# A Fourier mixing and feed-forward kernel: the head's loads, its d=128 transform and its weight products in another order

## The chip, the cores and the metric

One Trainium2 chip (trn2), one of its cores. The metric is the device time of one execution in microseconds, as the median of several runs. A profiled execution gives the spans, the rows and the waits that this text reads.

## What is computed

```python
def _attn_ref(x):                       # x: (8, 3008, 256) float32
    X = np.fft.fft(x, axis=1)
    X = np.fft.fft(X, axis=2)
    return X.real.astype(np.float32)

def _moe_ref(x, w_in, w_out):           # x: (24064, 256), w_in: (256, 2048), w_out: (2048, 256)
    h = x @ w_in
    g = np.maximum(0.01 * h, h)
    return (g @ w_out).astype(np.float32)
```

The real part of a two-dimensional Fourier transform of each batch goes, as 24064 rows of 256, through a layer of 2048 hidden units with a leaky ReLU and back to 256. `w_in` and `w_out` come as 64-bit floats, and the kernel makes 32-bit floats of them itself.

## The kernel before

**The mathematics.** The transform over the 256 features is never carried out on the data. It is multiplied into the first weights: `fold_w_in` makes `wf`, the product of a cosine and sine table (`feat_sb`) with `w_in`, in two halves, `wf[:, 0]` for the cosines and `wf[:, 1]` for the sines. Row 0 of the sine half holds the weights of feature 128, the nyquist feature of the feature axis (the "d=128" column); `spread_wn` sends these by small DMAs to `wn`, one column for each 128 hidden units. The transform over the 3008 sequence positions uses all its symmetries: the input is laid out with mirrored rows, `add_mirrors`, `fold_columns` and `fold_halves` add and subtract them on VectorE, and for even frequencies `fold_quarters` folds once more. What is left is a short product with a table (`sequence`: four matmuls of even rows into `pe`, three of odd rows into `po`), and `butterfly` puts the two sums together on ScalarE and VectorE as a tile `mix`.

**The units.** A unit is a batch and a parity of the frequency (odd first). Each has two mixes, block 0 for the cosines and block 1 for the sines; `dft` makes one. The d=128 column of all eight batches has a transform of its own (`nyquist`), with 8 rows instead of 128; its result is kept in DRAM and spread to all partitions by `spread`, or for the first unit by two matmuls with a row of ones (`spread_first`).

**The steps.** A unit's columns come in three blocks `j` of 251 or 250. `up(j, f)` multiplies two blocks of 128 hidden units (four matmuls into `cos_ps` and `sin_ps`), adds the d=128 column (L543), forms both signs (L547, L548) and applies the leaky ReLU (L549). `down` multiplies by `w_out`, with seven products instead of eight by a Strassen-Winograd scheme (L601), or plainly in the first two blocks (`down_plain`, L581). Here `f` runs over 8 pairs of hidden blocks. In the first two blocks the pair is `(2f, 2f+1)`, so that the steps need `wf` in rising order of columns.

**The head.** The first 16 steps are written out by hand, since they run while the weights still arrive. `load_w_in` and `load_w_out` issue loads on SP; `Weights.begin`, `mantissa` and `end` turn 64-bit words into 32-bit floats on VectorE (L343, L344, L351, L361, L362) with two steps on ScalarE (L345, L346); `convert_on(old, new)` runs the end of one conversion with the beginning of the next. `fold_w_in` is called five times: columns 0 to 255, 256 to 511, then three times 512 columns (`WN`). Each call makes the sine half's product first (L393), copies it on ScalarE (L394), issues the rows of `wn` (L401), then the cosine half's. `keep_warm(n)` issues `n` matmuls on a tile of zeros.

**What sets the order.** Inside the `with` block the order on VectorE, TensorE and SP is the one written, and in the inner block that of POOL too; ScalarE's is chosen by a scheduler when the program is built. After the block the scheduler orders all engines, by the order written and by what its own model takes to be ready, and it may put such later instructions between those of the block: the small quarter folds of the d=128 column (L274 to L280 on `nyx`), which are written after the block, stand on VectorE near 15 us. Loads share one queue on SP. Eight semaphores count their landings in turn, so a load also waits for the landing of the eighth before it. The PSUM tag `up` has four banks, used in turn by up steps, transforms and weight products; the tag `sum` has four for the down steps and the warming matmuls.

The lines that the prediction follows: L393 and L394 (weight products and copies), L401 (rows of `wn`), L431 and L441 (even and odd rows of a transform), L482 to L484 (the d=128 fold on POOL), L538 (up), L581 (plain down).

Of the kernel before, what the change touches and what calls it, by code (L numbers as in the profile page):

```python
# [48 lines left out]
F32 = mybir.dt.float32  # L49
# [6 lines left out]
P = 128  # L56
# [3 lines left out]
NT = 7  # L60
# [144 lines left out]
def tile_fnet_leaky_relu(  # L205
# [98 lines left out]

    def load_tab(q, n, c):
        t = const.tile([P, TW[c][n % 2]], F32, name=f"tab_{n}_{c}")
        q.dma_start(t, seq_tab[n, c, :, 0 : TW[c][n % 2]])
        tabs[n, c] = t
# [78 lines left out]

    def fold_w_in(f0, n, made):

        for w in (1, 0):  # L390
            pt = up_ps()[:, 0:n]
            for a in range(2):
                nc.tensor.matmul(pt, lhsT=feat_sb[:, a, w * P : (w + 1) * P], rhs=made[a].dst, start=(a == 0), stop=(a == 1))  # L393
            nc.scalar.copy(wf[:, w, f0 : f0 + n], pt)  # L394
            if w == 1:
                spread_wn(f0, n)
# [18 lines left out]

    def sequence(rows, m, part, c):

        pe, po = dft_ps(), dft_ps()  # L420
        kf, kw = KF[c], KW[c]
        tab, n = tabs[2 * part, c], NI[0]
        for i in range(n):
            if c == 1:
                still, to = rows[0:PE_ROWS, i], pe[0:m, i % 2 * kf : (i % 2 + 1) * kf]
            else:
                q, p = divmod(i, 2)
                still, to = rows[0][(p + part) % 2][0:PE_ROWS, q], pe[0:m, q * kf + p : (q + 1) * kf : 2]
            at = i * TW[c][0] // n

            nc.tensor.matmul(to, lhsT=still, rhs=tab[0:PE_ROWS, at : at + to.shape[1]],  # L431
                             start=(i == 0), stop=(i == n - 1), skip_group_check=True)
        tab, n, at = tabs[2 * part + 1, c], NI[1], 0
        for i in range(n):
# [8 lines left out]
            at += to.shape[1]  # L443
        return pe, po

# [12 lines left out]

    def dft(u, blk):


        b, c = u
        if u in folded:
            rows = folded[u][blk]
        elif c == 1:
            rows = zs[b][:, 1 - blk, 0, :, blk * P : (blk + 1) * P]
        else:
            rows = quarters.pop((b, blk))
        sums = sequence(rows, P, blk, c)

        def rest():
            t = work.tile([P, UW[0]], F32, tag=f"mix{blk}", bufs=2, name=f"mix{blk}")
            butterfly(t, sums, P, blk, c)
            mixed.setdefault(u, {})[blk] = t
        return rest

# [8 lines left out]

    def nyquist(c):
        if c == 1:
            rows = nya[:, 1]
        else:
            halves = [nyb[:, 0], nyb[:, 1]]  # L490
            fold_quarters(nya[:, 0], halves, halves[0][:, 5], [h[:, 6] for h in halves])
            rows = halves, halves[0][:, 5]
        sums = sequence(rows, B, 0, c)

        def rest():
            t = work.tile([P, UW[0]], F32, tag="mix0", bufs=2, name="nyq")
            butterfly(t, sums, B, 0, c)
            nc.sync.dma_start(nyq_dram[:, c, 0 : UW[c]], t[0:B, 0 : UW[c]])
            return t
        return rest  # L500

# [115 lines left out]
    def step(at):  # L617
        if at < len(steps):
# [6 lines left out]
            if n == 0 and f in (2, 5):  # L625
                dft(units[1], f // 5)()
            if 0 < n < len(units) - 1 and f == 4:
                if part == 0:
                    spread(units[n + 1])
                    if n % 2 == 1:  # L630
                        fold_x(b + 1)
                else:
                    dft(units[n + 1], part - 1)()
            if n % 2 == 0 and part == 2 and f == 6 and b + 1 < B:
# [5 lines left out]
    xs = {}  # L640

    def convert_w_in(f0, n, made):
        convert(made)
        fold_w_in(f0, n, made)

# [6 lines left out]
    with tc.manual_schedule(engines={mybir.EngineType.DVE, mybir.EngineType.PE, mybir.EngineType.SP}):  # L652
        with tc.manual_schedule(engines={mybir.EngineType.Pool}):
# [56 lines left out]
        for n in range(4):  # L710
            load_tab(nc.sync, n, 0)
        up(*steps[1])
# [4 lines left out]
        down_plain(*steps[1], halves=(0,))  # L717
        fold_w_in(half, half, w)
        convert_on(o1, w1[0])
# [9 lines left out]
        down_plain(*steps[3], halves=(0,))  # L729
        fold_w_in(WN, WN, w1)  # L730
        convert_on(o2, o3)
# [63 lines left out]
```

## Time and profile before

| what | us |
|---|---|
| median of 5 runs | 1933.27 (1931.32 to 1933.87) |
| the profiled execution's own time | 1933.27 |
| its span, first to last instruction | 1931.1 |
| TensorE busy | 1918.6 |
| VectorE busy | 1157.1 |
| first up step (L538) on TensorE | 29.33 |
| first plain down step (L581) | 34.26 |
| weight products (L393) on TensorE, starts | 10.28, 39.44, 52.25, 71.90, 96.66 |
| even rows of the d=128 column, second parity (L431 on nyx) | 121.51 |

All times inside an execution count from its first instruction. A line of the timeline gives start, duration, engine, line, operation, output and inputs, shapes, how many instructions were merged into it, and in brackets the engine's idle time before it and what ended that. A float32 matmul shows as two records, so four matmuls are "x8". The chain is the work that ended last, followed back from the last instruction.

### The profile page before, as it was taken

What the parts mean: (1) busy time and instruction counts of PE and PEld (TensorE: products, weight loads), DVE (VectorE), ACT (ScalarE), POOL (GpSimd) and SP (SyncE); (2) the same over time, 40 slices, a digit from 0 to 9 for tenths busy, and PEclk for the clock granted to TensorE, in tenths of its full rate; (3) what the DMA queues carried; (4) which work ended last, traced back from release to release, by engine and by line L of the source; (5) the groups of instructions that cost most, each with busy time, mean ns of one, the idle gap of its engine ahead of it and who ended that gap; (6) DMA issues with size and microseconds to landing.
All of it is one profiled execution on the core that took longest, in us unless ns stands there. A gap on an engine that the chain in (4) does not pass through costs nothing.

```text
span 1931.1 us, 24800 instructions
## 1 busy us (share of the span) xinstructions
PE 1918.6 (99%) x9040; PEld 1693.1 (88%) x9040; DVE 1157.1 (60%) x2273; ACT 468.6 (24%) x552; POOL 1062.0 (55%) x1513
## 2 busy tenths in 40 slices
PE   8999999999999999999999999999999999999999
PEld 6788888888888888888888888888888888888888
DVE  7868555584555755567555675558655585555554
ACT  3532222222222222222222222222222222222221
POOL 0136555575555755557555665556655565555554
PEclk9999999999999999999999999999999999999999
DMA  6202000010002000020000200002000020000000
GB/s 247 77 31 95 11 20 22 33 74 11 20 22 88 19 12 30 12 95 12 22 19 11 95 23 11 19 11 95 22 11 19 11 106 11 19 11 22 11 12 22
DMA packets 26729, 73.29 MB, mean 38 GB/s; under 512 B 4833, under 2 KB 17761, under 8 KB 24817
## 3 DMA queue, kind: packets, MB, share of 16 engines
q1 hardware_dynamic: 26608, 71.72, 10.0%
q8 instruction: 72, 1.18, 0.3%
q14 instruction: 49, 0.39, 0.1%
HBM read 46.99 MB, written 24.71 MB: 37 GB/s over the span
## 4 chain that ended last, share of the span: by engine, by line
PE 95%; DVE 3%; DMA 1%; issue 1%; SPq 0%; ACT 0%; DVEq 0%; ACTq 0%
PE sum_ps L601 55%; PE cos_ps L538 16%; PE sin_ps L538 16%; PE dft_ps L441 3%; PE sum_ps L581 3%; PE dft_ps L431 2%; DMA xt<-in_x_dram 1%; PE up_ps L393 1%; DVE cos L543 0%; DVE g L547 0%; DVE xt L241 0%; DVE g L548 0%; DVE xt L257 0%; DVE xt L247 0%; DVE xt L249 0%
## 5 line engine op out<-in xcount | busy, mean ns | idle before, releaser
L543 DVE SCALAR_TENSOR_TENSOR cos<-nb,wn,cos_ps 128x251 f32<-128x251 f32 (+1 forms) x768 | 330.3, 471 | 675.3 <-PE cos_ps L538 674.9
L549 ACT ACTIVATE g<-g 128x1004 f32<-128x1004 f32 (+1 forms) x384 | 399.2, 1040 | 1195.7 <-DVE g L548 1109.2
L556 POOL TENSOR_TENSOR s<-g 128x251 f32<-128x251 f32 (+1 forms) x368 | 268.9, 731 | 735.3 <-ACT g L549 735.1
L601 PE MATMUL sum_ps<-s,wt 128*128 128x251 f32 (+1 forms) x2208 | 528.0, 374 | 0.0
L601 PEld LDWEIGHTS sum_ps<-s,wt 128*128 128x128 f32 x2208 | 415.6, 188 | 53.2 <-issue 0.7
L538 PE MATMUL cos_ps<-mix,wf 128*128 128x251 f32 (+1 forms) x1536 | 388.4, 375 | 2.6 <-ACT wf L394 2.6
L538 PE MATMUL sin_ps<-mix,wf 128*128 128x251 f32 (+1 forms) x1536 | 387.8, 374 | 0.0
L601 PE MATMUL sum_ps<-g,wo 128*128 128x251 f32 (+1 forms) x1472 | 372.0, 374 | 0.9 <-DVE o L612 0.8
L538 PEld LDWEIGHTS cos_ps<-mix,wf 128*128 128x128 f32 x1536 | 290.8, 190 | 40.1 <-ACT wf L394 5.5
L538 PEld LDWEIGHTS sin_ps<-mix,wf 128*128 128x128 f32 x1536 | 290.4, 189 | 34.7
L601 PEld LDWEIGHTS sum_ps<-g,wo 128*128 128x128 f32 x1472 | 279.2, 190 | 40.6 <-DVE o L612 1.7
L559 POOL TENSOR_TENSOR s<-g,s 128x251 f32<-128x251 f32 (+1 forms) x368 | 272.2, 740 | 28.9
L547 DVE TENSOR_TENSOR g<-cos,sin_ps 128x502 f32<-128x502 f32 (+1 forms) x384 | 259.4, 676 | 47.0 <-DVE cos L543 12.8
L557 POOL TENSOR_TENSOR s<-s,g 128x251 f32<-128x251 f32 (+1 forms) x368 | 280.0, 761 | 0.0
L558 POOL TENSOR_TENSOR s<-g 128x251 f32<-128x251 f32 (+1 forms) x368 | 259.1, 704 | 0.0
L548 DVE TENSOR_TENSOR g<-cos,sin_ps 128x502 f32<-128x502 f32 (+1 forms) x384 | 257.0, 669 | 0.0
L601 PE MATMUL sum_ps<-g,wt 128*128 128x251 f32 (+1 forms) x736 | 215.8, 375 | 0.0
L601 PE MATMUL sum_ps<-s,wo 128*128 128x251 f32 (+1 forms) x736 | 215.8, 375 | 0.0
L601 PEld LDWEIGHTS sum_ps<-s,wo 128*128 128x128 f32 x736 | 139.5, 189 | 16.3
L601 PEld LDWEIGHTS sum_ps<-g,wt 128*128 128x128 f32 x736 | 139.8, 190 | 15.8
L612 DVE TENSOR_TENSOR o<-e,sum_ps 128x251 f32<-128x251 f32 (+1 forms) x184 | 67.4, 407 | 8.7 <-ACT e L610 8.7
L581 PE MATMUL sum_ps<-g,wo 128*128 128x251 f32 x256 | 57.1, 374 | 0.0
(75 smaller groups left out, 678.1 us busy)
## 6 DMA issues: line engine op xcount, KB each, us to landing
xt<-in_x_dram SPq DMA_DIRECT2D x14, 1792.0 KB, 9.1
out_dram<-o SPq DMA_DIRECT2D x80, 251.0 KB, 2.3
raw<-in_w_out_dram SPq DMA_DIRECT2D x8, 512.0 KB, 4.5
out_dram<-o SPq DMA_DIRECT2D x16, 250.0 KB, 2.1
raw<-in_w_in_dram SPq DMA_DIRECT2D x6, 512.0 KB, 4.7
nb<-nyq_dram SPq DMA_DIRECT2D x8, 376.5 KB, 3.5
nb<-nyq_dram SPq DMA_DIRECT2D x7, 376.0 KB
xt<-in_x_dram SPq DMA_DIRECT2D x2, 1024.0 KB, 8.9
```

The lines of the kernel that those rows point to most:

```text
L538: nc.tensor.matmul(pt[blk][:, h * n : (h + 1) * n], lhsT=wf[:, blk, fs[h] * P : (fs[h] + 1) * P], rhs=mixed[b, c][blk][:, at : at + n], st ...
L543: nc.vector.scalar_tensor_tensor(cos[:, hs], in0=spreads[b, c][:, at : at + n], scalar=wn[:, fs[h] : fs[h] + 1], in1=pt[0][:, hs], op0=ALU ...
L547: nc.vector.tensor_tensor(g[:, 0], cos[:, 0 : 2 * n], pt[1][:, 0 : 2 * n], op=ALU.add)
L548: nc.vector.tensor_tensor(g[:, 1], cos[:, 0 : 2 * n], pt[1][:, 0 : 2 * n], op=ALU.subtract)
L549: nc.scalar.activation(g, g, ACT.Lrelu)
L556: nc.gpsimd.tensor_tensor(s1, a[1][0], a[1][1], op=ALU.add)
L557: nc.gpsimd.tensor_tensor(s2, s1, a[0][0], op=ALU.subtract)
L558: nc.gpsimd.tensor_tensor(s3, a[0][0], a[1][0], op=ALU.subtract)
L559: nc.gpsimd.tensor_tensor(s4, a[0][1], s2, op=ALU.subtract)
L581: nc.tensor.matmul(sums[j][d][:, r * n : (r + 1) * n], lhsT=wo[:, fs[h] // NH, fs[h] % NH, d * P : (d + 1) * P], rhs=a[r][h], start=(f == ...
L601: nc.tensor.matmul(sums[j][p], lhsT=still[p], rhs=moving[p], start=(f == 0 and i % 2 == 0), stop=(f == NH - 1), skip_group_check=True)
L612: nc.vector.tensor_tensor(to, x, y, op=ALU.add)
```

## The change

It orders the first loads anew: both even halves of x, the first table and the d=128 column come ahead of the feature table, and three tables come behind the odd rows. `sequence` is split into `even_rows` and `odd_rows`, and `dft` and `nyquist` into their rows, products and mixes. The first weight product moves on TensorE from before the folds to between the even and the odd rows of the first transforms, and takes its banks from the tag `sum`. The sine columns of the even rows are folded ahead of the odd rows. The warming matmuls (10 and 7) become 20 at the start. The second and third weight products make the cosine half in two pieces, each copied by itself. The fourth is written one down step earlier, the fifth ahead of the down step of step 11 instead of before step 12. The two folds for even frequencies are both written in step 14, and the quarter folds of the first unit and of the d=128 column move into the block whose order on VectorE is fixed.

```diff
-    def fold_w_in(f0, n, made):
+    def fold_w_in(f0, n, made, tag="up", pieces=1):
         for w in (1, 0):
-            pt = up_ps()[:, 0:n]
-            for a in range(2):
-                nc.tensor.matmul(pt, lhsT=feat_sb[:, a, w * P : (w + 1) * P], rhs=made[a].dst, start=(a == 0), stop=(a == 1))
-            nc.scalar.copy(wf[:, w, f0 : f0 + n], pt)
+            m = n // (1 if w else pieces)
+            for at in range(0, n, m):
+                pt = ps.tile([P, 512], F32, tag=tag, bufs=4, name="wf_ps")[:, 0:m]
+                for a in range(2):
+                    nc.tensor.matmul(pt, lhsT=feat_sb[:, a, w * P : (w + 1) * P], rhs=made[a].dst[:, at : at + m],
+                                     start=(a == 0), stop=(a == 1))
+                nc.scalar.copy(wf[:, w, f0 + at : f0 + at + m], pt)
             if w == 1:
                 spread_wn(f0, n)
...
-    def sequence(rows, m, part, c):
-        pe, po = dft_ps(), dft_ps()
+    def even_rows(rows, m, part, c):
+        pe, kf = dft_ps(), KF[c]
...
+        return pe
+
+    def odd_rows(rows, m, part, c):
+        po, kw = dft_ps(), KW[c]
...
+    def nyquist_rows(c):
         if c == 1:
-            rows = nya[:, 1]
-        else:
-            halves = [nyb[:, 0], nyb[:, 1]]
-            fold_quarters(nya[:, 0], halves, halves[0][:, 5], [h[:, 6] for h in halves])
-            rows = halves, halves[0][:, 5]
-        sums = sequence(rows, B, 0, c)
...
+            return nya[:, 1]
+        halves = [nyb[:, 0], nyb[:, 1]]
+        fold_quarters(nya[:, 0], halves, halves[0][:, 5], [h[:, 6] for h in halves])
+        return halves, halves[0][:, 5]
+
+    def mix_nyquist(c, sums):
+        t = work.tile([P, UW[0]], F32, tag="mix0", bufs=2, name="nyq")
+        butterfly(t, sums, B, 0, c)
+        nc.sync.dma_start(nyq_dram[:, c, 0 : UW[c]], t[0:B, 0 : UW[c]])
+        return t
...
             w = load_w_in(0, half)
-            load_rows(0, evens)
+            for h in range(2):
+                load_rows(h, evens)
+            load_tab(0, 1)
+            nc.sync.dma_start(nyx, x_nyq)
             nc.sync.dma_start(feat_sb, feat_tab.rearrange("(a p) n -> p a n", p=P))
-            load_rows(1, evens)
-            nc.sync.dma_start(nyx, x_nyq)
-            for n in range(2):
-                load_tab(nc.sync, n, 1)
             for h in range(2):
                 load_rows(h, odds)
-            for n in range(2, 4):
-                load_tab(nc.sync, n, 1)
+            for n in range(1, 4):
+                load_tab(n, 1)
             o = load_w_out(0)
-            keep_warm(10)
             fold_nyquist()
-            convert_w_in(0, half, w)
-            w, w1 = load_w_in(half, half), load_w_in(WN, WN)
-            keep_warm(7)
+            convert(w)
...
-            nyq = nyquist(1)
+            folded[units[0]] = differences, t[:, 0, 0, :, P:D]
             for rows in (evens, odds):
                 for h in range(2):
                     add_mirrors(t, h, rows)
                     fold_columns(t, h, 0, rows)
                     if rows == odds and h == 0:
-                        fold_columns(t, h, 1, slice(0, NT))
+                        fold_columns(t, h, 1, rows)
                 fold_halves(t, 0, 1, rows, differences)
-            fold_columns(t, 1, 1, slice(0, NT))
+                for h in range(2):
+                    if rows == evens or h == 1:
+                        fold_columns(t, h, 1, rows)
             fold_halves(t, 1, 1, slice(0, NT))
             zs[0] = t
-            folded[units[0]] = differences, t[:, 0, 0, :, P:D]
-            ready = [nyq, dft(units[0], 0), dft(units[0], 1)]
-            spread_first(ready[0]())
-            ready[1]()
+            keep_warm(20)
+            cosine, sine = ((rows_of(units[0], blk), P, blk, 1) for blk in range(2))
+            nyq = nyquist_rows(1), B, 0, 1
+            evens = [even_rows(*nyq), even_rows(*cosine)]
+            fold_w_in(0, half, w, "sum")
+            w, w1 = load_w_in(half, half), load_w_in(WN, WN)
+            sums_of_d128 = evens[0], odd_rows(*nyq)
+            sums_of_cosines = evens[1], odd_rows(*cosine)
+            sums_of_sines = even_rows(*sine), odd_rows(*sine)
+            spread_first(mix_nyquist(1, sums_of_d128))
+            mix(units[0], 0, sums_of_cosines)
             o.begin()
             o.mantissa()
-            ready[2]()
+            mix(units[0], 1, sums_of_sines)
...
-        fold_w_in(half, half, w)
+        fold_w_in(half, half, w, pieces=2)
...
-        fold_w_in(WN, WN, w1)
+        fold_w_in(WN, WN, w1, pieces=2)
...
         up(*steps[7])
+        fold_w_in(2 * WN, WN, w2)
         down(*steps[5])
-        fold_w_in(2 * WN, WN, w2)
...
-            if at == 12:
-                fold_w_in(3 * WN, WN, w3)
             if old is not None:
                 convert_on(old, new)
             up(*steps[at])
+            if at == 11:
+                fold_w_in(3 * WN, WN, w3)
             down(*steps[at - 2])
-            if at > 13:
-                fold_halves(t, at - 14, 0, slice(0, NT))
+            if at == 14:
+                for part in range(2):
+                    fold_halves(t, part, 0, slice(0, NT))
         done = 14
-    for part in range(2):
-        fold_x_quarters(0, part)
-    nyquist(0)()
+        for part in range(2):
+            fold_x_quarters(0, part)
+        nyq = nyquist_rows(0), B, 0, 0
+    mix_nyquist(0, (even_rows(*nyq), odd_rows(*nyq)))
     spread(units[1])
```

More of the change, by code (lines that the diff above doesn't have):

```diff
@@ L303, in tile_fnet_leaky_relu, with load_tab @@
     tabs = {}
-    def load_tab(q, n, c):
+    def load_tab(n, c):
         t = const.tile([P, TW[c][n % 2]], F32, name=f"tab_{n}_{c}")
-        q.dma_start(t, seq_tab[n, c, :, 0 : TW[c][n % 2]])
+        nc.sync.dma_start(t, seq_tab[n, c, :, 0 : TW[c][n % 2]])
         tabs[n, c] = t
@@ L414, in combine_w_out @@
             nc.gpsimd.tensor_tensor(to, x, y, op=ALU.subtract)
-    def sequence(rows, m, part, c):
-        pe, po = dft_ps(), dft_ps()
-        kf, kw = KF[c], KW[c]
+    def even_rows(rows, m, part, c):
+        pe, kf = dft_ps(), KF[c]
         tab, n = tabs[2 * part, c], NI[0]
@@ L443, in sequence @@
             at += to.shape[1]
-        return pe, po
+        return po
     def butterfly(t, sums, m, part, c):
@@ L457, in butterfly, with rows_of, mix, dft @@
         nc.vector.tensor_tensor(t[0:m, kw : UW[c]], ev[0:m, 0:rest], po[0:m, 0:rest], op=ALU.subtract)
-    def dft(u, blk):
+    def rows_of(u, blk):
         b, c = u
         if u in folded:
-            rows = folded[u][blk]
-        elif c == 1:
-            rows = zs[b][:, 1 - blk, 0, :, blk * P : (blk + 1) * P]
-        else:
[L468 to L475, printed above, removed]
+            return folded[u][blk]
+        if c == 1:
+            return zs[b][:, 1 - blk, 0, :, blk * P : (blk + 1) * P]
+        return quarters.pop((b, blk))
+    def mix(u, blk, sums):
+        t = work.tile([P, UW[0]], F32, tag=f"mix{blk}", bufs=2, name=f"mix{blk}")
+        butterfly(t, sums, P, blk, u[1])
+        mixed.setdefault(u, {})[blk] = t
+    def dft(u, blk):
+        args = rows_of(u, blk), P, blk, u[1]
+        mix(u, blk, (even_rows(*args), odd_rows(*args)))
     nyq_dram = dram.tile([B, 2, UW[0]], F32, name="nyq_dram")
@@ L484, in fold_nyquist @@
         nc.gpsimd.tensor_tensor(nya[:, 0], nyb[:, 0], nyb[:, 1], op=ALU.add)
-    def nyquist(c):
+    def nyquist_rows(c):
         if c == 1:
-            rows = nya[:, 1]
-        else:
-            halves = [nyb[:, 0], nyb[:, 1]]
-            fold_quarters(nya[:, 0], halves, halves[0][:, 5], [h[:, 6] for h in halves])
-            rows = halves, halves[0][:, 5]
-        sums = sequence(rows, B, 0, c)
[L495 to L500, printed above, removed]
+            return nya[:, 1]
[7 more added lines that the diff above has]
+        return t
     def spread(u):
@@ L625, in step @@
             if n == 0 and f in (2, 5):
-                dft(units[1], f // 5)()
+                dft(units[1], f // 5)
             if 0 < n < len(units) - 1 and f == 4:
@@ L632, in step @@
                 else:
-                    dft(units[n + 1], part - 1)()
+                    dft(units[n + 1], part - 1)
             if n % 2 == 0 and part == 2 and f == 6 and b + 1 < B:
@@ L640, in tile_fnet_leaky_relu @@
     xs = {}
-    def convert_w_in(f0, n, made):
-        convert(made)
-        fold_w_in(f0, n, made)
     def keep_warm(n):
@@ L710, in tile_fnet_leaky_relu @@
         for n in range(4):
-            load_tab(nc.sync, n, 0)
+            load_tab(n, 0)
         up(*steps[1])
```

## The prediction

> **What bounds the kernel now.** I read the page first, then the chain of waits in order of time, then the timeline from 0 to 125 us, and last the busy time by stretches around the first 22 us.
>
> The page, its first section and the chain's shares by engine:
>
> ```profile
> PE 1918.6 (99%) x9040; PEld 1693.1 (88%) x9040; DVE 1157.1 (60%) x2273; ACT 468.6 (24%) x552; POOL 1062.0 (55%) x1513
> ...
> PE 95%; DVE 3%; DMA 1%; issue 1%; SPq 0%; ACT 0%; DVEq 0%; ACTq 0%
> ```
>
> TensorE sets the end. Its real products are the same number before and after, so the time moves only by what TensorE waits for in the head, the first 125 us. The end of the kernel is shifted and not reshaped.
>
> The chain in order of time shows which waits these are:
>
> ```profile
> 6.21 10.90 DMA xt<-in_x_dram
> ...
> 52.41 3.45 PE up_ps L393 x8
> 55.86 0.02 issue
> 55.88 0.59 ACT wf L394
> 56.48 0.04 issue
> 56.52 1.11 PE cos_ps L538 x4
> ```
>
> Up to 17.1 the odd rows of x are awaited. Later each weight product (L393) is followed by a hole in which ScalarE copies it out (L394) before the next up step can start: 0.62 us at 41.95 and 0.67 to 0.68 at 56.52, 76.17 and 100.93 by the timeline's idle column. Matmul start to matmul start, the three large ones are 0.84 us over the 427 ns pitch of 512 columns, and at most 0.1 of that remains without the wait.
>
> The timeline, for the places that the change touches (start, duration, engine, line, idle before):
>
> ```profile
> 10.28 2.67 PE L393 MATMUL up_ps<-win,feat_sb 128*128 128x256 f32 x8 [2.90 <-DMA feat_sb<-in_feat_tab_dram]
> ...
> 13.04 1.12 POOL L482 TENSOR_TENSOR nyx<-nyx 128x112 f32<-128x112 f32 x1 [11.87 <-DMA nyx<-in_x_nyq_dram]
> 14.24 0.30 POOL L483 TENSOR_TENSOR nyx<-nyx 128x56 f32<-128x56 f32 x1
> ...
> 16.88 1.44 PE L431 MATMUL dft_ps<-tab,nyx 95*8 95x188 f32 x8
> ...
> 29.33 1.11 PE L538 MATMUL cos_ps<-mix,wf 128*128 128x251 f32 x4
> ...
> 57.67 0.86 DVE L543 SCALAR_TENSOR_TENSOR cos<-nb,wn,cos_ps 128x251 f32<-128x251 f32 x2 [2.41 <-PE cos_ps L538]
> ...
> 68.50 3.56 PE L581 MATMUL sum_ps<-g,wo 128*128 128x251 f32 x16
> ...
> 71.33 0.69 DVE L362 SCALAR_TENSOR_TENSOR win<-win,power 128x512 f32<-128x512 f32 x1
> ...
> 71.90 3.60 PE L393 MATMUL up_ps<-win,feat_sb 128*128 128x512 f32 x8
> ```
>
> The first weight product sits in a time when TensorE has nothing else. The third is fed at 72.02, just as TensorE arrives. The stretches (busy TensorE second, granted clock third from the end):
>
> ```profile
> 8.00:11.30 3.30, 1.02 (x5) 0.95 (x6) 1.84 (x2) 0.00 (x0) 0.00 (x0) 1.00 1.02 404
> 11.40:14.70 3.30, 3.30 (x9) 2.61 (x9) 1.23 (x1) 0.74 (x2) 1.58 (x3) 0.50 1.02 413
> ```
>
> **Part A, the start (likely +0.3 us).** The DMA engines move about 0.41 MB per us here, so landings shift with the bytes ahead of them. The 256 KB of the feature table no longer lie ahead of the second even half: 12.66 becomes 12.0. The odd rows lose the 564 KB table from ahead of them: 17.14 becomes 15.75. The nyquist column (13.04) gets 376 KB of table ahead and loses 256 KB: 13.25. VectorE's folds gain: of each 1.08 us L249 row about half is now done while the odd rows are awaited, so the fold of the halves that ended at 23.92 ends near 21.5, and the small nyquist folds (L274 to L280, some 0.7 us, with 0.95 idle before them) leave this stretch. VectorE alone could begin the first up step 2.4 us earlier, at 28.1 for 30.55.
>
> TensorE cannot follow. Its transforms may start when POOL has folded the nyquist column: 13.25 + 1.5 = 14.75, and with the release 14.85, against 16.88 before. Behind that now lie in order: even rows of d=128 (1.28), of the cosines (1.38), the weight product (8 matmuls at 216 ns, 1.75), the odd rows (1.89 and 1.98), both sine parts (1.35 and 1.90), the spread (1.37); 12.9 us, each from its start-to-start times in the timeline, and some 0.6 of releases between groups. The first up step is then at 14.85 + 13.5 = 28.35, for 29.33: a gain of 1.0 at full clock.
>
> The clock: 40 warming matmuls start at 1.10; the first 20 end at 7.2, 20 more at 216 ns end near 11.6. So TensorE idles about 3.2 us before 14.85. Before the change it idled 2.90 us (7.4 to 10.28), and the next stretch, 11.40 to 14.70, ran at 0.50. I take the same to happen: matmuls at twice the pitch for up to 3.4 us, which costs 0 to 1.7 us. I take 1.3, near the upper end, since that row is the nearest there is. The first up step is at 29.65, +0.3, with ends of -1.0 and +0.7.
>
> The Trainium skill's page "TensorE: Matmul & The Clock Gate", section "Part 1: The HAM clock gate", puts the drop only after at least one idle window of about 3.4 us. By that rule a gap of 3.2 us would leave the clock up, Part A would be -1.0 and the whole sum -0.25 us. This case's row differs, because a gap of 2.90 us was enough. The same section says that the window is free-running, so the loss may differ between executions, which no run here shows.
>
> Other work in this part is covered. The late table (564 KB) lands near 19, and the odd rows of d=128 come at 19.5 or later. Sine even rows need the PSUM bank that VectorE frees at 22.0, and TensorE is there at 23.5. The up step waits for the second sine sum, done near 28. On SP the two small rows of L401, the four next weight loads and the nyquist store stand behind the copy of the first product, now near 18.6 to 20.7 (it was 11.8). The loads are issued near 20 to 23 for 15.27 to 20.0, land at 24 to 28, and are first read at about 30 (L343 at 29.98 before).
>
> **Part B, the second product, in pieces of 128 (likely -0.4).** Of the 0.62 idle, the copy is behind a 0.72 us power step on ScalarE. Two short copies overlap the second piece's 0.43 us. Ends 0 and -0.65.
>
> **Part C, the third, pieces of 256 (likely -0.55).** The up step reads only the first piece, whose copy lies beside the second's matmuls (0.86). It can be caught behind the power step of 0.72 at 55.07. Ends -0.3 and -0.75. Columns per matmul are halved and their number doubled, at a pitch that falls with the columns (216 ns at 256, 427 at 512), so no TensorE time is added.
>
> **Part D, the product at 72, moved ahead of one down step (likely +1.95).** It needs the last conversion of its weights, VectorE's L362 that ends at 72.02. VectorE's queue has no idle time from 57.67 to there: three up steps and three conversions. That string starts with the up step at 56.52 and ends 15.5 us later, wherever it starts. TensorE reaches the new place at 68.66, 12.14 after that up step. One half of the first product (0.86) can run, then it waits from 13.0 to 15.5, some 2.5 us, and the down step's 3.40 us, which covered this, is queued behind. After the wait 2.58 of product and 3.40 of down put the next up step at 21.6 after 56.52, where it was 19.65. The hole for the copy is gone and is in this figure. Ends +1.7 and +2.2.
>
> **Part E, the last product, one step earlier (likely -0.75).** Its weights are ready at 92.36 (L362 91.67 + 0.69) and TensorE gets there at 93.26, so nothing waits. Ends -0.84 and -0.6.
>
> **Part F, the quarter folds at the end of the head (likely +0.5).** In VectorE's fixed order they now come after the last up step's g (119.6): two parts of 1.66 and 0.7 for the nyquist column. TensorE finds the nyquist rows ready at 123.1 instead of 121.51. If its queue has them first, it waits 1.6; if the next up step was put ahead, it waits 0. I take a third.
>
> **Sum.** 0.3 - 0.4 - 0.55 + 1.95 - 0.75 + 0.5 = +1.05 us. The profiled execution took 1933.27 (span 1931.1 and 2.2 around it), which is also the median of the five runs, so 1934.3.
>
> **Rivals.** *Clock kept, transform not late* (25%): A at -1.0, F at 0: -1.0 - 0.4 - 0.55 + 1.95 - 0.75 = -0.75, 1932.5. For it: the gap is only just as long as the one seen. Against it: that one was shorter.
>
> *VectorE sets the pace* (7%): the first up step follows the folds, -2.3, and the conversion comes in time in Part D, so that all four holes close (-0.4 and three times -0.75): -4.95, 1928.3. Against it: 12.9 us of listed TensorE work and 14.3 us of VectorE rows without idle time.
>
> *Weight loads late* (11%, slower): SP's loads behind the first product decide if the first lands after about 30. Before, landing took 6.2 to 8.1 us in a busy queue. From an issue at 22 that is 28 to 30; another 3 us of lateness would hold VectorE, the second product and all behind it one for one: 1934.3 + 3 = 1937.3 and beyond.
>
> **How the numbers follow.** The forecast has 57%, the rivals 25, 7 and 11. A measurement of this kernel can tell about 0.2% from no change, 3.9 us. The forecast and the first rival lie inside it, so same has 0.82, faster 0.07, slower 0.11. Adding all low ends (-1.0 - 0.65 - 0.75 + 1.7 - 0.84 + 0) gives -1.5, all high ones (+0.7 + 0 - 0.3 + 2.2 - 0.6 + 1.6) +3.6: the forecast's own range is 1931.8 to 1936.9. The range goes from -2.3, part of the way to the VectorE case, to +3.0, where all high ends at once are unlikely: 1931.0 to 1937.3.
>
> **What would show it.** Part A is right if the first nyquist matmul is near 14.85 at a pitch of 318 ns (159 at full clock) and the first up step is within 28.3 to 30.1. Part D is right if L393 of the 1024th column idles some 2.5 us on VectorE's L362, before L581. Parts B, C and E are right if no up step shows a wait for L394 over 0.3 us. Part F shows at L431 on nyx near 121. It is wrong if L538 first starts before 27, or if TensorE waits on w_in data.

## The result and the profile after

The kernel after takes 1936.5 us (median of 27 runs, 1932.0 to 1940.4), the one before 1932.5 (47 runs, 1930.1 to 1933.9). The ratio is 1.0020 [1.0014, 1.0025], or +3.9 us [2.7, 4.8]. The median lies inside the predicted range and 2.9 us above the sum of +1.05. It is on the 0.2% line that the prediction drew as the edge of what can be told, but the interval excludes a ratio of 1. Measured once more on another chip (after_again below) the same kernel was +2.1 us [0.4, 3.9] over before, so the sum was short by 1.1 to 2.9. The profiled execution took 1935.39 us (span 1933.2), 2.12 more than the one of before; the rows below explain those 2.12, and the rest of the median is a matter of other executions of the same kernel. The spread is more than twice that of before.

The page of after, its first section and the chain's shares by engine:

```profile
PE 1920.9 (99%) x9054; PEld 1695.4 (88%) x9054; DVE 1157.1 (60%) x2275; ACT 468.2 (24%) x554; POOL 1062.4 (55%) x1515
...
PE 95%; DVE 2%; DMA 1%; issue 1%; ACT 0%; SPq 0%; POOL 0%; DVEq 0%; ACTq 0%; POOLq 0%
```

TensorE still sets the end. Its busy time rose by 2.3 us with 14 more matmul records (two for each matmul): 8 come with the pieces and add no columns, 6 are three more warming matmuls. The page alone does not tell whether the rest of the work ran at its old speed; the rows below do.

The timeline of TensorE, kernel after (start, duration, engine, line, idle before and who ended it). Product rows are L396 now, up steps L543, down steps L586:

```profile
14.97 1.44 PE L434 MATMUL dft_ps<-tab,nyx 95*8 95x188 f32 x8 [2.07 <-POOL nyx L491]
...
28.25 1.11 PE L543 MATMUL cos_ps<-mix,wf 128*128 128x251 f32 x4
...
54.28 1.01 PE L543 MATMUL cos_ps<-mix,wf 128*128 128x251 f32 x4
...
61.08 3.67 PE L586 MATMUL sum_ps<-g,wo 128*128 128x251 f32 x16 [1.54 <-ACT g L554]
...
68.13 1.13 PE L396 MATMUL wf_ps<-win,feat_sb 128*128 128x512 f32 x2
72.10 4.40 PE L396 MATMUL wf_ps<-win,feat_sb 128*128 128x512 f32 x6 [2.85 <-DVE win L362]
76.34 3.56 PE L586 MATMUL sum_ps<-g,wo 128*128 128x251 f32 x16
79.74 1.01 PE L543 MATMUL cos_ps<-mix,wf 128*128 128x251 f32 x4
...
125.61 0.82 PE L434 MATMUL dft_ps<-tab,nyx 95*8 95x95 f32 x8 [0.23 <-DVE nyx L274]
```

Two rows of before that the comparison needs and that are not shown above:

```profile
76.17 1.11 PE L538 MATMUL cos_ps<-mix,wf 128*128 128x251 f32 x4 [0.68 <-ACT wf L394]
...
179.64 1.11 PE L601 MATMUL sum_ps<-g,wo 128*128 128x251 f32 x4 [0.76 <-DVE o L612]
```

Compare the starts. First up step: 28.25 for 29.33 (-1.08). The one after the third product: 54.28 for 56.52 (-2.24), so the pieces of Parts B and C brought another 1.16. After the fourth product: 79.74 for 76.17, so +3.57. Between those two rows 5.8 us were lost, and the two idle notes say where: 1.54 at 61.08, where TensorE waits for g, and 2.85 at 72.10, where it waits for the conversion in L362, as foretold. Behind them the moved last product gives back 0.94 (its up step at 103.56 for 100.93, so +2.63), and a wait of 0.76 that TensorE had at 179.64 before is gone; the span ends at +2.1. The row at 72.10 carries a second sign: its six records take 4.40 us, where 6 x 0.427 and the pipeline's tail would be some 2.8 (2.84 in wn_free, below).

The busy time by stretches of after gives the granted clock (third from the end; busy TensorE is second):

```profile
12.00:15.00 3.00, 0.93 (x6) 0.48 (x5) 2.93 (x4) 0.00 (x0) 1.66 (x3) 1.00 1.04 418
71.90:75.20 3.30, 3.10 (x4) 1.51 (x5) 3.20 (x8) 1.32 (x3) 0.00 (x0) 0.50 0.83 272
```

Here the gap in the head did not lower the clock, and the stall in front of the fourth product did. The first is what the rival "clock kept" said of Part A; the second stands in no part of the prediction.

VectorE's timeline of after shows why TensorE waited for g at 61.08:

```profile
57.72 0.86 DVE L548 SCALAR_TENSOR_TENSOR cos<-nb,wn,cos_ps 128x251 f32<-128x251 f32 x2 [3.87 <-DMA wn<-wf]
...
71.35 0.69 DVE L362 SCALAR_TENSOR_TENSOR win<-win,power 128x512 f32<-128x512 f32 x1
```

The row before started at 57.67 and was released by TensorE (L538). Now it starts at 57.72 and is released by a DMA: four rows of 128 values that SP copies out of the product's sine half, the half that is made first (tile wn, L405). TensorE came 2.24 earlier, VectorE not at all. All that Parts A, B and C had brought was lost at this row, and the conversion of the fourth product ended at 72.04 as it had at 72.02.

### The profile page after: what moved, and what is told of

Read it like the earlier page. It is cut to its first block, busy times and chain, and to the rows that moved or that the text cites. A ratio compares the mean times of both kernels' runs of the same rounds, so it can differ in the third digit from the quotient of the medians.

```text
span 1933.2 us, 24832 instructions
## 1 busy us (share of the span) xinstructions
PE 1920.9 (99%) x9054; PEld 1695.4 (88%) x9054; DVE 1157.1 (60%) x2275; ACT 468.2 (24%) x554; POOL 1062.4 (55%) x1515
## 4 chain that ended last, share of the span: by engine, by line
PE 95%; DVE 2%; DMA 1%; issue 1%; ACT 0%; SPq 0%; POOL 0%; DVEq 0%; ACTq 0%; POOLq 0%
PE sum_ps L606 54%; PE cos_ps L543 16%; PE sin_ps L543 16%; PE dft_ps L449 3%; PE sum_ps L586 3%; PE dft_ps L434 2%; DMA xt<-in_x_dram 1%; PE wf_ps L396 1%; DMA nyx<-in_x_nyq_dram 1%; DVE g L552 0%; DVE g L553 0%; DVE cos L548 0%; DVE xt L257 0%; DVE xt L241 0%; DVE xt L249 0%
## 5 line engine op out<-in xcount | busy, mean ns | idle before, releaser
L543 PE MATMUL cos_ps<-mix,wf 128*128 128x251 f32 (+1 forms) x1536 | 388.4, 375 | 0.1
L543 PE MATMUL sin_ps<-mix,wf 128*128 128x251 f32 (+1 forms) x1536 | 387.8, 374 | 0.0
L543 PEld LDWEIGHTS cos_ps<-mix,wf 128*128 128x128 f32 x1536 | 291.0, 190 | 35.3 <-issue 0.6
L543 PEld LDWEIGHTS sin_ps<-mix,wf 128*128 128x128 f32 x1536 | 290.4, 189 | 34.7
L586 PE MATMUL sum_ps<-g,wo 128*128 128x251 f32 x256 | 57.2, 375 | 1.5 <-ACT g L554 1.5
```

The costliest lines, as they stand in the source:

```text
L543: nc.tensor.matmul(pt[blk][:, h * n : (h + 1) * n], lhsT=wf[:, blk, fs[h] * P : (fs[h] + 1) * P], rhs=mixed[b, c][blk][:, at : at + n], st ...
L586: nc.tensor.matmul(sums[j][d][:, r * n : (r + 1) * n], lhsT=wo[:, fs[h] // NH, fs[h] % NH, d * P : (d + 1) * P], rhs=a[r][h], start=(f == ...
```

## The experiments

**First group: which part costs the time.** The theory was that the moved fourth product costs all of it; the rivals were the new start, the small rows of wn and the quarter folds. Four kernels shared one chip and one set of runs of before (1932.6).

*d_back*: the kernel after, with the fourth product back behind the down step.

```diff
         up(*steps[7])
-        fold_w_in(2 * WN, WN, w2)
         down(*steps[5])
+        fold_w_in(2 * WN, WN, w2)
```

> The changed kernel with the fourth weight product put back behind the down step of step 5; nothing else differs. Theory: the stall in front of that product (2.85 us of TensorE idle on VectorE's L362 in the profile of after) and the half clock that follows it (0.50 from 71.9 to 75.3) are the loss and also the spread of 8 us between executions. Then the median falls by 3 to 4.5 us to about 1932 to 1933.5, TensorE does not wait for L362 at the product, and the executions lie within 3 us like those of before. Rival: the loss and the spread come from the new start (TensorE idle 2.1 us between the warming matmuls and the transforms, at a clock that differs between executions). Then the median stays above 1935 and the spread stays near 8 us.

*d_only*: the kernel before, with the same two lines the other way round: Part D by itself.

> The kernel before with one edit: the fourth weight product is written ahead of the down step of step 5. Theory: TensorE waits 2.5 us for L362, the clock drops to half for one stretch or more, and the time rises by 2.5 to 5 us over before, with a spread of several us. Rival (the start is the cause): no more than 1 us over before, with the spread of before.

*wn_free*: the kernel after, with the up steps that follow the third product reading column 0 of wn, which has long been there (so these steps add the d=128 weights of another hidden block).

```diff
-   scalar=wn[:, fs[h] : fs[h] + 1],
+   scalar=wn[:, 0:1] if j < plain and f == 2 else wn[:, fs[h] : fs[h] + 1],
```

> The changed kernel, but the up steps with f = 2 of the first two column blocks take column 0 of wn, which landed long before, instead of the columns 4 and 5 that the third product has just sent; two hidden blocks of two column blocks get a wrong d=128 weight. Theory: in the profile of after VectorE waited 3.87 us for those rows (landing at 57.6, behind an instruction fetch), which used up all that the head had gained by then. Without that wait the string of up steps and conversions on VectorE starts 2 us earlier, the fourth product is still stalled by 2.5 to 3 us, and the end comes 1.5 to 2.5 us earlier than after. Rival: the wait is no part of the path, or was an accident of the one profile: same median as after within 0.5 us.

*f_back*: the kernel after, with the quarter folds and the nyquist rows outside the hand-written order again.

```diff
-        for part in range(2):
-            fold_x_quarters(0, part)
-        nyq = nyquist_rows(0), B, 0, 0
+    for part in range(2):
+        fold_x_quarters(0, part)
+    nyq = nyquist_rows(0), B, 0, 0
```

> The changed kernel with the quarter folds of the first unit and of the d=128 column written behind the block again, so that the scheduler places them. Theory: in the profile of after TensorE waited only 0.4 us at the d=128 rows (three matmuls of the next down step had been put ahead), so the median moves by 0 to -0.6 us; the small folds stand again near 15 us on VectorE and cost nothing there, since TensorE sets the pace. Rival: Part F of the prediction at its high end: -1.6 us.

| kernel | median (lowest to highest), us | ratio to before |
|---|---|---|
| d_back | 1931.06 (1928.47 to 1934.01) | 0.9994 [0.9985, 1.0003] |
| d_only | 1935.62 (1934.18 to 1937.90) | 1.0016 [1.0008, 1.0025] |
| wn_free | 1935.08 (1928.77 to 1936.49) | 1.0008 [0.9999, 1.0016] |
| f_back | 1933.44 (1930.73 to 1938.54) | 1.0006 [0.9998, 1.0015] |

Part D costs +3.1 us [1.5, 4.8] alone on the kernel before. Without it the rest of the change is at -1.2 us [-2.9, +0.6]. The other two are spread over 8 us and tell little by their medians; their profiles tell more, but they are of single executions: wn_free's is the fastest of its twelve (1928.77), f_back's the slowest of its eleven (1938.54). In wn_free TensorE no longer waits for g behind the third product, though a row landed late there as well (3.5 us from issue to landing); so the rows of wn are what it had waited for in after. d_back's runs lie 5.5 us apart, where 3 was expected, so the new start has a share in the spread: that is the second group. The timelines of TensorE around the fourth product, first d_only:

```profile
67.51 1.02 PE L393 MATMUL up_ps<-win,feat_sb 128*128 128x512 f32 x2
71.06 4.54 PE L393 MATMUL up_ps<-win,feat_sb 128*128 128x512 f32 x6 [2.53 <-DVE win L362]
...
78.84 1.01 PE L538 MATMUL cos_ps<-mix,wf 128*128 128x251 f32 x4
```

then wn_free:

```profile
64.37 1.02 PE L396 MATMUL wf_ps<-win,feat_sb 128*128 128x512 f32 x2
67.92 2.84 PE L396 MATMUL wf_ps<-win,feat_sb 128*128 128x512 f32 x6 [2.53 <-DVE win L362]
...
74.00 1.01 PE L543 MATMUL cos_ps<-mix,wf 128*128 128x251 f32 x4
```

and f_back:

```profile
70.79 1.13 PE L396 MATMUL wf_ps<-win,feat_sb 128*128 128x512 f32 x2
74.76 5.49 PE L396 MATMUL wf_ps<-win,feat_sb 128*128 128x512 f32 x6 [2.84 <-DVE win L362]
...
83.68 1.01 PE L543 MATMUL cos_ps<-mix,wf 128*128 128x251 f32 x4
```

The same 2.53 us of idleness stand in the first two, and the six records behind them take 4.54 us in one and 2.84 in the other. Their granted clocks in the busy time by stretches, d_only and then wn_free:

```profile
71.20:74.50 3.30, 3.30 (x4) 1.38 (x5) 3.20 (x8) 1.32 (x2) 0.00 (x0) 0.50 0.87 308
```

```profile
68.00:71.30 3.30, 3.30 (x10) 1.80 (x11) 3.20 (x8) 1.89 (x4) 0.00 (x0) 1.00 0.93 309
```

So the price of Part D at its place has two terms. From the end of the seventh up step to the start of the next up step it was 7.67 us before (68.50 to 76.17). It is 9.63 in wn_free, with the clock kept: +1.96, the predicted +1.95. It is 11.33 in d_only and 11.61 in after, with one stretch at half clock (+3.66 and +3.94), and 12.89 in f_back, whose clock stayed at 0.50 from 73.68 to 80.5 (+5.2). At half clock 3.4 us are worth 1.7, 6.8 are worth 3.4. Some of it comes back: d_only, like after, has no wait left near 180, where before waited 0.76.

d_only holds a second drop, in its head, behind a shorter gap. TensorE waits 1.89 us for VectorE, and the next matmuls run at half clock (from 19.90 to 23.31):

```profile
20.05 3.75 PE L441 MATMUL dft_ps<-tab,differences 128*128 128x376 f32 x6 [1.89 <-DVE differences L257]
```

```profile
20.00:23.20 3.20, 3.15 (x5) 1.85 (x6) 2.99 (x6) 0.00 (x0) 0.00 (x0) 0.50 1.05 419
```

The gap of 2.07 us in the head of after did not do that. So the length of a gap alone does not decide; the last section comes back to it.

**Second group: the head and the small rows.** The open questions were why the times of one kernel lie so far apart, what Part A does alone, and whether the rows of wn can be had sooner. Before measured 1932.42 beside these four.

*after_again* is the kernel after, unchanged. *warm24* is d_back with four more warming matmuls, which make 48 records for 40:

```diff
-            keep_warm(20)
+            keep_warm(24)
```

*wn_early* is warm24 with the sine half of the product in pieces too, and the rows of wn sent behind each piece:

```diff
-            m = n // (1 if w else pieces)
+            m = n // pieces
...
-            if w == 1:
-                spread_wn(f0, n)
+                if w == 1:
+                    spread_wn(f0 + at, m)
```

*head_only* is Part A by itself: the kernel after with the products in one piece, both moved products at their old places and the quarter folds outside.

> The changed kernel once more, on one chip beside the next three, for its times and a second profile. Two states of the clock in the head are behind its spread: d_back had executions at 1928.5 to 1929.6 (mean clock 1.000), near 1931 (0.999) and at 1933.4 to 1934.0 (0.998). Theory: the same three groups plus the stall in front of the fourth product, so 1932 to 1933.5, 1934 to 1935.5 and 1936.5 to 1939. Rival: one group only.

> The changed kernel with two edits: the fourth product back behind its down step (as in d_back), and 24 warming matmuls for 20, so that TensorE idles some 1.7 us less before the first transform. Theory: in d_back's profile the clock was 0.50 from 15.4 to 22.2 us, right after an idle stretch of 3.4 us, and this is what makes d_back's slower groups (two windows of 3.4 us at half clock are 3.4 us of TensorE work, and 1931 is one window). With the gap at 1.7 us or less the clock stays up in nearly every execution: median 1928.5 to 1929.5, lowest as in d_back, spread under 2 us. Rival (the groups come from something else than the idle gap, DMA landings for example): median near 1931 and the same spread.

> warm24 with one more edit: in the second and third product the sine half is made in two pieces too, and the rows of wn are sent after each piece's copy. Theory: the up step behind the third product waits on VectorE for the rows of wn, since the hole for ScalarE's copy was gone before their landing (57.7 in the profile of after; TensorE then idles 1.0 to 1.5 us for the g of that step). The first two rows are issued about 1 us earlier, so 0.5 to 1.2 us less than warm24, and TensorE's idle before the second down step shrinks by as much. Rival (a landing is held by other traffic, an instruction fetch of 16 KB seen at 55.6, and not by its issue): no change within 0.3 us.

> Part A alone: the changed kernel's start (loads, folds, split transforms, first product between even and odd rows, 20 warming matmuls), and everything after it as before: products in one piece at their old places, quarter folds left to the scheduler. Theory: executions at full clock are 1.0 us faster than the fastest of before (1930.1), so 1929.1; those that run the transforms at half clock are 2.5 us slower than that, so the median is 1930.5 to 1932.5 and the spread 3 to 5 us. Prediction's Part A: +0.3 on the median, 1932.9. Rival: the start is bound by loads as before, no change at full clock.

| kernel | median (lowest to highest), us | ratio to before |
|---|---|---|
| after_again | 1934.33 (1932.92 to 1936.63) | 1.0011 [1.0002, 1.0020] |
| warm24 | 1928.84 (1927.66 to 1929.98) | 0.9981 [0.9972, 0.9990] |
| wn_early | 1929.54 (1928.36 to 1930.64) | 0.9983 [0.9975, 0.9992] |
| head_only | 1933.43 (1929.91 to 1934.32) | 0.9998 [0.9990, 1.0007] |

TensorE's timelines of the head, d_back first, then warm24:

```profile
14.99 2.31 PE L434 MATMUL dft_ps<-tab,nyx 95*8 95x188 f32 x8 [2.99 <-POOL nyx L491]
...
19.89 3.05 PE L396 MATMUL wf_ps<-win,feat_sb 128*128 128x256 f32 x8
...
31.59 1.11 PE L543 MATMUL cos_ps<-mix,wf 128*128 128x251 f32 x4
```

```profile
1.10 12.63 PE L651 MATMUL sum_ps<-blank 128*128 128x256 f32 x48 [1.10 <-POOL blank L656]
13.65 1.44 PE L434 MATMUL dft_ps<-tab,nyx 95*8 95x188 f32 x8
...
26.94 1.11 PE L543 MATMUL cos_ps<-mix,wf 128*128 128x251 f32 x4
```

and their granted clocks, d_back and warm24:

```profile
15.50:22.10 6.60, 6.60 (x20) 4.98 (x19) 6.39 (x11) 1.27 (x5) 0.42 (x5) 0.50 0.71 285
```

```profile
5.30:1900.00 1894.70, 1893.54 (x8955) 1674.02 (x8954) 1147.28 (x2251) 462.12 (x547) 1052.03 (x1496) 1.00 0.10 38
```

From the first nyquist matmul to the first up step it is 13.28 us in after, 13.29 in warm24, and 16.60 in d_back: +3.3, which is half of 6.6 to 6.8 us at 0.50. The profiles fall into two kinds by the idle time ahead of the nyquist matmuls. With 2.89 to 2.99 (d_back, f_back, and 2.96 in head_only) all took 16.6; with 2.07 and less (after, after_again, wn_free, warm24) all took 13.3.

Why one kernel has gaps of different lengths can be read from the warming row, d_back first, then after:

```profile
1.10 10.89 PE L651 MATMUL sum_ps<-blank 128*128 128x256 f32 x40 [1.10 <-POOL blank L656]
```

```profile
1.10 11.80 PE L651 MATMUL sum_ps<-blank 128*128 128x256 f32 x40 [1.10 <-POOL blank L656]
```

Warming records come 427 ns apart until the clock first rises, and 216 ns apart from then on. The trace puts that rise at 5.17 us in d_back and at 7.01 in after, so the same 40 records end 0.9 us later in after. The nyquist column landed alike in the two (13.32 and 13.27), and the gap is shorter by what the warming took longer. Where the column lands early, the gap is short too (11.60 in wn_free, gap 0.80).

Closing the gap is enough: d_back's eleven runs lie in groups at mean clocks of 1.000 (1928.5 to 1929.6), 0.999 (1930.9 to 1933.3) and 0.998 (1933.4 to 1934.0); warm24 has 1927.7 to 1930.0, d_back's first group, and the clock stays at 1.00 up to the end. The two ran on different chips; against its own before d_back is at -1.2 us and warm24 at -3.7. The runs of after fall into groups in the same way: 1932.0 to 1935.4 at a mean clock of 0.999, 1933.6 to 1937.2 at 0.998, 1937.0 to 1940.4 at 0.997 and 0.996.

wn_early brought nothing; its median is 0.7 above warm24's. Its VectorE waits for TensorE at that row, not for wn, and starts at 54.39, where warm24 starts at 54.47; its third product lasts 0.21 us longer from its start to the up step (3.65 for 3.44). In warm24 VectorE does wait for the rows, some 0.5 us, but TensorE has no idle time behind it. So an earlier issue is worth nothing in these two executions; whether it would help in one with late rows was not tried. VectorE's timeline in d_back (late) and warm24 (early enough):

```profile
59.12 0.47 DVE L548 SCALAR_TENSOR_TENSOR cos<-nb,wn,cos_ps 128x251 f32<-128x251 f32 x1 [1.95 <-DMA wn<-wf]
60.89 0.48 DVE L548 SCALAR_TENSOR_TENSOR cos<-nb,wn,cos_ps 128x251 f32<-128x251 f32 x1 [1.29 <-DMA wn<-wf]
```

```profile
54.47 1.08 DVE L548 SCALAR_TENSOR_TENSOR cos<-nb,wn,cos_ps 128x251 f32<-128x251 f32 x2 [1.94 <-DMA wn<-wf]
```

In d_back one of the four rows lands 1.3 us late and TensorE idles 0.99 for the next g. Every profile has one 16 KB instruction packet near here; what differs is when it starts. In d_back it starts at 58.66, with the rows issued from 57.1 to 58.9, and the slowest row needs 3.2 us from issue to landing. In warm24 it starts at 51.05, ahead of the first issue at 52.5, and the slowest needs 2.1. All 14 profiles go that way: in nine the packet starts after the first row's issue, and the slowest row takes 3.1 to 3.8 us; in five it starts 1 us or more ahead of it (warm24, wn_early, w_fourth_pieces, w_folds_back, w_last_late), and the slowest takes 2.0 to 2.1. That the packet is what holds a row up fits this, but no run moved the packet alone. A late row costs TensorE something only where VectorE is waiting for it: in before, d_only, head_only and w_one_piece a row is late too, and VectorE still waits for TensorE there.

**Third group: the smaller parts, with the clock steady.** All four start from warm24, which varies by 2.3 us only. Before measured 1932.52 beside them. They ran on another chip than warm24, so I take a difference to warm24 as good to about 1 us, and the last column is no more than a guide; the rows show more.

```diff
# w_fourth_pieces: the fourth product in two pieces, at its old place
-        fold_w_in(2 * WN, WN, w2)
+        fold_w_in(2 * WN, WN, w2, pieces=2)
# w_folds_back: the quarter folds outside again, as in f_back
# w_one_piece: the second and third product in one piece
-        fold_w_in(half, half, w, pieces=2)
+        fold_w_in(half, half, w)
-        fold_w_in(WN, WN, w1, pieces=2)
+        fold_w_in(WN, WN, w1)
# w_last_late: the last product ahead of up step 12, as before the change
```

> warm24 (1928.84, spread 2.3) with the fourth product's cosine half in two pieces, at its place behind the down step. Theory: the one hole for ScalarE's copy that is left there (0.99 us between L396 and L543 in warm24's profile) closes, -0.5 to -0.9: 1928.0 to 1928.4. Rival (the rows of wn are late, as at the third product in the profile of after): the idle time moves to the next down step, no change within 0.3 us.

> warm24 with the quarter folds and the d=128 folds left to the scheduler again: Part F by itself, now that the spread is small. Theory: -0.4 to -0.6 us, the wait of TensorE at the d=128 rows near 118.8 (0.40 us over the pitch in warm24) and its release. Rival: the small folds near 15 us hold VectorE in the head, where d_back's VectorE is idle for TensorE anyway: no cost, so no rival there; the prediction's middle of Part F was -0.5, its high end -1.6.

> warm24 with the second and third product in one piece each: Parts B and C by themselves. Theory: both holes come back, +0.4 and +0.55 to +0.8: 1929.8 to 1930.0. Rival: what the pieces win is lost again to the wait for wn and to the second release of ScalarE (0.25 us inside the up step of the second product): within 0.3 us of warm24.

> warm24 with the last product before the up step of step 12 again: Part E by itself. Theory: the hole of 0.84 us comes back, +0.75: 1929.6. Rival: some other wait behind it absorbs it (the 0.4 us at the d=128 rows, the start of the seven products near 175), under +0.3.

| kernel | median (lowest to highest), us | ratio to before | to warm24, us |
|---|---|---|---|
| w_fourth_pieces | 1928.13 (1927.31 to 1928.94) | 0.9976 [0.9967, 0.9985] | -0.7 |
| w_folds_back | 1927.77 (1927.39 to 1929.21) | 0.9975 [0.9965, 0.9985] | -1.1 |
| w_one_piece | 1930.22 (1929.46 to 1930.76) | 0.9988 [0.9979, 0.9997] | +1.4 |
| w_last_late | 1929.74 (1928.90 to 1930.93) | 0.9987 [0.9978, 0.9996] | +0.9 |

The holes are back where the pieces and the move are undone. TensorE's timeline of w_one_piece, and then of w_last_late:

```profile
40.39 1.11 PE L543 MATMUL cos_ps<-mix,wf 128*128 128x251 f32 x4 [0.61 <-ACT wf L398]
...
54.95 1.11 PE L543 MATMUL cos_ps<-mix,wf 128*128 128x251 f32 x4 [0.68 <-ACT wf L398]
```

```profile
98.43 1.11 PE L543 MATMUL cos_ps<-mix,wf 128*128 128x251 f32 x4 [0.68 <-ACT wf L398]
```

In w_fourth_pieces the up step behind the fourth product has no idle note at 72.23, where warm24 waits 0.83 for L398 at 72.78. w_folds_back is the fastest kernel of this study, 4.8 us [2.9, 6.8] ahead of before by its ratio. Its trace does not tell all of the 1.1 us: from the first up step to the end of the span it takes 1898.55 us, warm24 takes 1898.56. So Part F costs between nothing and 1.1, and the trace does not show that it costs anything.

## Why the prediction was right, and which of its steps was not

The direction came out, and the median lies in the range; the sum was short, +1.05 for +3.9. Two terms left the clock out or took it too small, and both err to the same side.

That the range held is in part luck. Its upper end is given as +3.0 and as 1937.3, but +3.0 on the 1933.27 of before is 1936.3; 1937.3 is +4.0, or +3.0 on top of the sum. The measured 1936.5 and +3.9 lie above the first and below the second. The 1933.27 itself, the median of five runs, is 0.8 above the median of the 47 runs.

**Part A (+0.3, from -1.0 to +0.7).** The order of work was right, and in after's profile the times too: 13.27 for the landing of the nyquist column (13.25 foretold), 14.97 for the first nyquist matmul (14.85), and 28.25 for the first up step where 28.35 was foretold at full clock. The agreement to a tenth is luck of that profile: with the same head the column landed at 12.44 in after_again and at 11.60 in wn_free, and the first up step came at 27.37 and 26.46, the latter ahead of the 27 that the prediction named as a sign of being wrong. The gap before the nyquist matmuls was taken as 3.2 us; it was 0.80 to 2.99, since the warming ended at 11.99 to 12.90 and not at 11.6, and the column landed at different times. The clock's part was mis-sized. I took one stretch of 3.4 us at half clock as the worst that a gap can cost, 1.7 us, since before showed one. The six profiles with this head and 20 warming matmuls show none or two: 0 or 3.3. Part A alone is -0.4 us [-1.9, +1.4] by its ratio and +1.0 by the medians. In single profiles the first up step stands at 26.5 to 28.3 with the clock kept and at 31.6 to 31.8 without, where the head of before has 28.4 (d_only) and 29.3.

**Part D (+1.95, 1.7 to 2.2).** This was the right mechanism at the right place. The string on VectorE took 15.4 us from the up step in wn_free (15.5 foretold), the stall was 2.53 (2.5) and the loss 1.96. The step that failed is that I priced the stall by its own length alone. In Part A I had called a gap of 2.9 us enough to halve the clock, and did not ask the same of this gap of 2.5. In after, after_again, d_only and f_back it was enough; in wn_free's profile it was not. In the profiles the clock's term is 1.7 or 3.3, enough for the 1.1 to 2.9 us by which the sum was short. d_only's median, +3.1 against the predicted +1.95, points the same way, but its interval of 1.5 to 4.8 holds 1.95; it is the rows that show the term apart from the rest.

The Trainium skill's page "TensorE: Matmul & The Clock Gate", section "Part 1: The HAM clock gate", asks for at least one idle window of about 3.4 us before the clock falls, and says that the windows are free-running. The first does not hold here: 2.53 us without a matmul, inside a stretch with work on both sides, halved the clock in d_only, and so did 1.89 us in its head. The second agrees: the clock's first rise, at 4.15 to 7.01 us, came at another time in each execution, and the same 2.53 us did not halve the clock in wn_free.

**Parts B and C (-0.4 and -0.55).** Undone together they cost 1.4 for the predicted 0.95, to about 1 us; the holes that come back are 0.61 and 0.68. The working left out who is late next: with the hole closed, VectorE's step waits for the rows of wn, whose landing was hidden before. In four of the profiles that took back 0.9 to 1.5 us of TensorE's time, in the five profiles with a steady clock and the pieces nothing.

**Part E (-0.75)**: undone it costs 0.9, to about 1 us, and the hole that comes back is 0.68. **Part F (+0.5, from 0 to 1.6)** lies in its range. TensorE's queue had three matmuls (six records) of the next down step ahead of the nyquist rows, and it waited 0.23 at 125.61: close to the second of the two cases, with matmuls of a down step and not the up step put ahead.

**The rivals.** *Weight loads late* is false: the loads behind the first product were issued at 20.4 to 22.1, landed by 27.5 and were first read at 27.86. *VectorE sets the pace* is false in the head; behind the third product VectorE did set the pace, but on a DMA. *Clock kept* describes Part A in three of the six profiles with the new head and no extra warming, but not the fourth product.

## What to carry to other kernels

Price a stall on TensorE twice: by its length, and by what the clock may do behind it. Here 1.9 to 3 us without a matmul cost up to 3.3 us more, in some executions and not in others, and four more warming matmuls took the toss out of the head and 2.2 to 2.5 us off the median. When a short wait is closed, look for the small transfer that it had hidden. One profile can agree with a forecast to a tenth by luck; take a second. When one kernel's times lie in groups, sort them by the mean granted clock before comparing medians.

## What the runs showed of the hardware that was not expected

A drop to half clock lasted one stretch (71.10 to 74.51 in d_only) or two (15.41 to 22.23 in d_back, 73.68 to 80.5 in f_back), although TensorE was busy throughout the second (6.60 of 6.60 us in d_back's row above). Which of the two follows stays open.

Where a drop can begin is regular. In all 14 traces the warming matmuls go from a pitch of 427 ns to 216 when the clock first rises, at 4.15 to 7.01 us, and all nine drops inside the kernel start a whole number of stretches of 3.413 us after that rise: 2 in before, 3 in d_back, 19 in after, 4 and 19 in d_only. So one and the same gap can fall into one such stretch or across the border of two. d_only's 2.53 us fall into one (67.68 to 71.10); wn_free's are divided, 2.00 before the border at 67.39 and 0.53 behind it. Seven gaps with 2.3 us or more in one stretch (2.31 of the 2.90 in before) were each followed by half clock, and none with 1.54 or less in each stretch was (the 2.07 in the head of after are 0.94 and 1.13). In between it goes both ways: 1.73 in d_only's head and 1.76 in f_back were followed by half clock, 2.00 in wn_free was not. So the place of a gap tells more than its length, but not all.
